# Issuing the first weight load of a decode block ahead of the opening barrier

## The chip, the cores and the metric

The kernel runs on one core of one Trainium2 chip. The metric is the device time of one execution, in microseconds. Times of one set of runs are compared only with the kernel before as it ran in the same set on the same chip.

A ratio of two kernels is the mean time of one kernel's runs over the mean of the other's in the same rounds.

## The reference

The program is one decode step (one token) of a transformer block: layer norm, grouped-query attention over a cache of 65,536 positions, a residual add, then layer norm, a gated GELU feed-forward and a second residual add. All weights and both caches are bfloat16 and are read once.

```python
def _A_ref(x, k_cache, v_cache, wq, wo):          # x is (1, 1, 1024)
    q = (x @ wq).reshape(1, 1, 32, 128).transpose(0, 2, 1, 3)
    k = jnp.repeat(k_cache, 8, axis=1)            # k_cache is (1, 4, 65536, 128)
    v = jnp.repeat(v_cache, 8, axis=1)
    scores = jnp.einsum("bhqd,bhkd->bhqk", q, k) * (128 ** -0.5)
    p = _softmax(scores, axis=-1)
    o = jnp.einsum("bhqk,bhkd->bhqd", p, v)
    return o.transpose(0, 2, 1, 3).reshape(1, 1, 4096) @ wo

def _B_ref(x, w_gate, w_up, w_down):              # 1024 -> 3584 -> 1024
    return (_gelu(x @ w_gate) * (x @ w_up)) @ w_down

h = x + _A_ref(_layernorm(x), A_k_cache, A_v_cache, A_wq, A_wo)
h2 = h + _B_ref(_layernorm(h), B_w_gate, B_w_up, B_w_down)
```

There are about 173 MB to read from HBM, the chip's main memory, and very little arithmetic for each byte.

## The kernel before

All large operands pass through five buffers of 4 MB. SyncE issues every one of these loads; ScalarE issues two small loads of `x`.

```python
    def load(src, name):
        t = chpool.tile([P, CW], BF16, name=name, tag="ch")      # 5 buffers, 128 x 16384 bf16
        n, w = src.shape[1], src.shape[2]
        tv = t[:, 0:n * w].rearrange("p (n w) -> p n w", w=w)
        nc.sync.dma_start(out=tv, in_=src)
        return tv
    # ... cut ...
    nc.scalar.dma_start(out=x_pc_bf[:], in_=A_x[0, 0].rearrange("(p c) -> p c", c=DC))   # 128 x 16 bytes
    nc.scalar.dma_start(out=x_row[:], in_=A_x[0, 0].rearrange("(g n) -> g n", g=4))
    wq_tiles = []
    for c0 in range(0, DC, WB):                                  # two loads of 4 MB
        wv = load(wq_v[:, c0:c0 + WB, :], "wq_sb")
        wq_tiles.extend(wv[:, i, :] for i in range(WB))
    # ... cut: constants, layer norm of x, q = x @ wq, then the K loads, the V loads and the rest ...
```

The kernel already has one build hook, a function that is called with the finished program before it is compiled and may edit its instruction lists (it drops repeated weight loads of TensorE). The change adds a second hook of this kind.

Ahead of the kernel's own instructions the framework puts an opening block. In it GpSimd writes four constants, and then all five engines meet at a barrier: each drains and reports to GpSimd, which releases them. SyncE's part of that block is, in order: drain and report; wait for the release; branch to the body. The first load is the first instruction of SyncE's body and waits for nothing.

## Time and profile before

| What | Value | Read from |
|---|---|---|
| Time, median of 3 runs | 409.46 us | runs |
| Span, first to last instruction | 407.74 us | profile |
| First weight packet starts | 1.76 us | packets in the trace |
| Last weight packet ends | 403.89 us | packets in the trace |
| Stream (the difference) | 402.13 us | |
| Tail after it | 3.84 us | |

A packet is one record of a DMA transfer in the trace; for most of the loads it is the 32 KB row of one partition. "Stream" and "tail" keep the meaning of this table throughout.

The page of the kernel before, its slices, DMA and queue lines. Each digit is the busy share of one fortieth of the span in tenths.

```profile
PE   0455287769998777797966969978767999725464
DVE  0218988876693679545454978181844000220110
DMA  8999999999999999999999999999999999999995
GB/s 360 412 450 424 420 453 411 457 415 447 426 415 460 415 442 428 418 456 415 456 416 421 450 415 455 418 434 437 418 453 418 452 421 431 428 434 436 422 429 222
...
q1 hardware_dynamic: 6488, 173.02, 98.6%
...
HBM read 173.02 MB, written 0.00 MB: 424 GB/s over the span
```

PE and DVE have room in most slices; DMA has none between the first slice and the last. Queue q1 is SyncE's loads.

The stretches table of the kernel before (time in each stretch, busy time and number of instructions of each engine, granted clock, DMA share, GB/s). A short stretch can read above the real rate, because the table books packets whole; so the first rows only show where the DMA starts.

```profile
0.00:1.00 1.00, 0.00 (x0) 0.00 (x0) 0.17 (x2) 0.00 (x0) 0.47 (x6) 1.00 0.00 0
1.00:1.70 0.70, 0.00 (x0) 0.00 (x0) 0.00 (x1) 0.00 (x0) 0.67 (x4) 1.00 0.00 0
1.70:2.70 1.00, 0.00 (x0) 0.00 (x0) 0.00 (x0) 0.90 (x1) 1.00 (x1) 1.00 1.75 524
...
25.00:100.00 75.00, 50.62 (x196) 11.46 (x100) 57.93 (x37) 11.42 (x18) 0.00 (x0) 0.78 1.00 433
100.00:200.00 100.00, 85.85 (x386) 15.26 (x154) 65.50 (x43) 11.53 (x16) 0.00 (x0) 0.98 1.00 432
200.00:300.00 100.00, 80.78 (x331) 13.91 (x131) 59.16 (x40) 11.40 (x16) 1.14 (x2) 0.90 1.00 433
```

No byte moves before 1.70 us, and from 25 us on the share is 1.00 at 432 to 433 GB/s. Counted packet by packet over all queues, the 16 engines were idle for at most 0.1 us per engine between 12 and 395 us. The Trainium skill, "DMA: Bandwidth & Descriptors", section "Where 436 GB/s comes from", puts the ceiling of the fabric at 435 GB/s; this trace is within 1% of it.

The chain of waits of the kernel before seems to tell another story:

```profile
DMA 45%; PE 30%; DVE 18%; ACT 4%; issue 2%; SPq 0%; ACTq 0%; DVEq 0%
```

It follows each load back to the instruction that freed its buffer, and so it wanders through PE and DVE. But such a wait only makes a load enter its queue later, and the queue is never empty: the K loads take 32.9 us from issue to landing (the page's list of issues), while a 4 MB load alone takes 4.19 MB / 432 GB/s = 9.7 us, so about three are queued. Counted from the issues and the packets, the bytes still waiting when a new load is issued are never less than 1.1 loads of 4 MB.

The start of the timeline of the kernel before (start us, us, engine, line, operation, out<-in, count, idle before and its cause; "SPq" and "ACTq" are the issues of SyncE and ScalarE):

```profile
0.24 0.10 POOL L523 MEMSET const-float32-0.0<- 128x1 f32 x1 [0.24 <-issue]
...
0.73 0.41 ACTq L149 DMA_DIRECT2D x_pc_bf<-in_A_x_dram  x1
0.73 0.20 POOL masks.py:197 MEMSET ident_bf<- 128x128 bf16 x1 [0.29 <-POOLq L523]
0.74 0.87 SPq L143 DMA_DIRECT2D wq_sb<-in_A_wq_dram  x2
...
13.07 0.17 DVE L195 CAST x_pc<-x_pc_bf 128x8 f32<-128x8 bf16 x1 [12.07 <-DMA x_pc_bf<-in_A_x_dram]
```

Nothing but constants runs before 0.73 us, when the barrier has let go and both queues issue their first load. The small `x` lands only at 13.07 us. The timeline leaves out the barrier itself; the records of the trace have it (ns from the first instruction):

```
   0  SyncE drains and reports      532  GpSimd has seen all reports
 121  VectorE drains and reports    653  SyncE sees the release
 132  ScalarE drains and reports    736  SyncE starts to issue the first load (393 ns)
 315  TensorE drains and reports   1760  the first packet of that load starts
```

### The profile page before, as it was taken

The page shows a single profiled execution, that of the slowest core. Times are in us where ns is not written, and L with a number is a line of the kernel's source. Part 1 is how long each engine was busy: PE and PEld are TensorE (multiplying, and loading weights), DVE is VectorE, ACT ScalarE, POOL GpSimd, SP SyncE. Part 2 cuts the span into 40 slices and gives each one's busy share as a digit, 9 for nine tenths or more (in the row PEclk, how much of TensorE's full clock was granted, in tenths as well). Part 3 has the DMA queues.
Part 4 walks back from the last instruction along what each step waited for, and adds up shares of the span by engine and source line. Part 5 has one row for each costly group of instructions (what it writes and reads, how often), then busy time and mean ns, then how long its engine had stood idle before and what let it go on. Part 6 is the DMA issues. An engine that isn't in the chain of part 4 may idle for free.

```text
span 407.7 us, 2657 instructions
## 1 busy us (share of the span) xinstructions
PE 298.5 (73%) x1481; PEld 62.8 (15%) x713; DVE 201.9 (50%) x183; ACT 44.9 (11%) x67; POOL 7.4 (2%) x17
## 2 busy tenths in 40 slices
PE   0455287769998777797966969978767999725464
PEld 0121011111111111111101121111112110200232
DVE  0218988876693679545454978181844000220110
ACT  1010000051000041000001420000042000100000
POOL 2000000000000000000000000000010000100000
PEclk9966868969999999899988798999678799875766
DMA  8999999999999999999999999999999999999995
GB/s 360 412 450 424 420 453 411 457 415 447 426 415 460 415 442 428 418 456 415 456 416 421 450 415 455 418 434 437 418 453 418 452 421 431 428 434 436 422 429 222
DMA packets 6652, 173.19 MB, mean 425 GB/s; under 512 B 872, under 2 KB 880, under 8 KB 1136
## 3 DMA queue, kind: packets, MB, share of 16 engines
q1 hardware_dynamic: 6488, 173.02, 98.6%
q8 instruction: 8, 0.13, 0.1%
q10 hardware_dynamic: 152, 0.00, 0.0%
q14 instruction: 4, 0.03, 0.0%
HBM read 173.02 MB, written 0.00 MB: 424 GB/s over the span
## 4 chain that ended last, share of the span: by engine, by line
DMA 45%; PE 30%; DVE 18%; ACT 4%; issue 2%; SPq 0%; ACTq 0%; DVEq 0%
DMA k_sb<-in_A_k_cache_dram 32%; DVE k_sb L255 12%; PE acc_ps L128 12%; DMA wg_sb<-in_B_w_gate_dram 8%; PE qk_ps L126 6%; PE qk_ps L128 6%; DMA wd_sb<-in_B_w_down_dram 5%; PE acc_ps L126 4%; DVE mx L276 2%; ACT sc L275 2%; DVE pT L300 1%; ACT pe_r L297 1%; PE o_ps L126 1%; DVE acc_sb L326 1%; ACT acc_sb L328 1%
## 5 line engine op out<-in xcount | busy, mean ns | idle before, releaser
L255 DVE STREAM_TRANSPOSE k_sb<-k_sb 128x2048 uint32<-128x2048 uint32 x64 | 142.1, 2277 | 33.5 <-DMA k_sb<-in_A_k_cache_dram 33.5
L126 PE MATMUL qk_ps<-k_sb,wsel 128*128 128x512 bf16 x256 | 104.2, 407 | 37.7 <-DVE k_sb L255 24.0
L128 PE MATMUL acc_ps<-v_sb,pT 128*128 128x512 bf16 x384 | 112.3, 404 | 0.0
L128 PE MATMUL qk_ps<-k_sb,wsel 128*128 128x512 bf16 x256 | 103.8, 405 | 0.0
L126 PE MATMUL acc_ps<-v_sb,pT 128*128 128x512 bf16 x128 | 51.8, 405 | 0.0
L126 PEld LDWEIGHTS <-wsel 128*128 128x128 bf16 x256 | 26.1, 102 | 142.7 <-issue 123.6
L276 DVE TENSOR_REDUCE mx<-qk_ps 128x1 f32<-128x1024 f32 x16 | 19.5, 1219 | 45.5 <-ACT sc L275 45.5
L275 ACT COPY sc<-qk_ps 128x1024 f32<-128x1024 f32 x16 | 16.2, 1012 | 202.0 <-PE qk_ps L128 201.9
L126 PEld LDWEIGHTS <-pT 128*128 128x128 bf16 x128 | 13.5, 106 | 99.3 <-issue 99.3
L300 DVE STREAM_TRANSPOSE pT<-pe_r 128x1024 bf16<-128x1024 bf16 x16 | 19.0, 1227 | 6.2 <-ACT pe_r L297 6.2
L326 DVE COPY acc_sb<-acc_ps 32x512 f32<-32x512 f32 x8 | 5.4, 671 | 32.9 <-PE acc_ps L128 32.9
L297 ACT ACTIVATE pe_r<-sc,nbias 128x1024 bf16<-128x1024 f32 x16 | 18.2, 1140 | 14.6 <-DVE nbias L292 13.9
L126 PE MATMUL ln_tot<-ln_s,ones_f 128*128 128x1 f32 x8 | 1.9, 311 | 16.1 <-DVE ln_s L176 14.2
L128 PE MATMUL wu_ps<-wu_sb,hnz 128*32 128x512 bf16 x40 | 7.3, 585 | 7.2 <-DMA wu_sb<-in_B_w_up_dram 7.2
L328 ACT COPY acc_sb<-acc_ps 32x512 f32<-32x512 f32 x8 | 4.6, 578 | 62.1 <-DVE acc_sb L326 62.1
L212 DVE COPY wg_ev<-wg_ps 128x512 f32<-128x512 f32 x1 | 0.7, 692 | 20.0 <-PE wg_ps L126 20.0
L126 PE MATMUL f_ps<-wd_sb,actz 128*32 128x256 bf16 x112 | 6.2, 377 | 5.7 <-DMA wd_sb<-in_B_w_down_dram 5.7
L126 PE MATMUL o_ps<-sel,acc_sb 128*128 128x8 f32 x32 | 5.0, 283 | 6.7 <-DVE rl L340 5.9
L126 PE MATMUL wg_ps<-wg_sb,hnz 128*32 128x512 bf16 x32 | 6.8, 621 | 4.3 <-DMA wg_sb<-in_B_w_gate_dram 2.8
L137 PE MATMUL mxT_ps<-ident_f,mx 128*1 128x128 f32 x4 | 1.4, 346 | 10.8 <-DVE mx L281 10.8
L126 PE MATMUL q_ps<-wq_sb,xnz 128*32 128x512 bf16 x32 | 4.5, 539 | 3.6 <-DMA wq_sb<-in_A_wq_dram 2.0
L126 PEld LDWEIGHTS <-hnz 128*32 128x32 bf16 x48 | 2.7, 129 | 23.4 <-issue 21.8
(100 smaller groups left out, 85.2 us busy)
## 6 DMA issues: line engine op xcount, KB each, us to landing
k_sb<-in_A_k_cache_dram SPq DMA_DIRECT2D x16, 4096.0 KB, 32.9
v_sb<-in_A_v_cache_dram SPq DMA_DIRECT2D x16, 4096.0 KB, 36.8
wq_sb<-in_A_wq_dram SPq DMA_DIRECT2D x2, 4096.0 KB, 16.7
wo_sb<-in_A_wo_dram SPq DMA_DIRECT2D x2, 4096.0 KB, 30.1
wg_sb<-in_B_w_gate_dram SPq DMA_DIRECT2D x2, 3584.0 KB, 31.2
wu_sb<-in_B_w_up_dram SPq DMA_DIRECT2D x2, 3584.0 KB, 32.2
wd_sb<-in_B_w_down_dram SPq DMA_DIRECT2D x1, 3584.0 KB
wd_sb<-in_B_w_down_dram SPq DMA_DIRECT2D x1, 1792.0 KB, 24.4
```

The source lines that it names most:

```text
L126: return pe(t.matmul(out, lhsT=lhsT, rhs=rhs, start=start, stop=stop, tile_position=tile_position, skip_group_check=skip_group_check))
L128: op = t.add_instruction(mybir.InstMatmult(name=nc.get_next_instruction_name(), engine=t.engine, start_tensor_calc=start, stop_tensor_calc ...
L137: pe(nc.tensor.transpose(out=out, in_=in_, identity=identity))
L212: nc.vector.tensor_copy(out=dst, in_=src)
L255: dv(nc.vector.transpose(out=kt[:, c * w:(c + 1) * w], in_=kt[:, c * w:(c + 1) * w]))
L275: ac(nc.scalar.copy(out=sc[:], in_=flat))
L276: dv(nc.vector.tensor_reduce(out=state[("mx", g)][:, li:li + 1], in_=flat, axis=AX.X, op=ALU.max))
L297: ac(nc.scalar.activation(out=pe_r[:], in_=state.pop(("sc", g, li))[:], func=ACT.Exp, bias=nbias[:, 0:1], scale=scale, accum_out=lpart[:, ...
L300: dv(nc.vector.transpose(out=pT[:].rearrange("p m c -> p (m c)"), in_=pe_r[:]))
L326: dv(nc.vector.tensor_copy(out=acc_sb[sl, :], in_=acc[sl, c, :]))
L328: ac(nc.scalar.copy(out=acc_sb[sl, :], in_=acc[sl, c, :]))
```

## The change

The intent is to let the DMA stream start while the engines are still meeting. The first load depends on nothing: its buffer is fresh and it waits for no semaphore. So a hook takes it out of the body and puts it ahead of SyncE's drain in the opening block.

```diff
+    SPE = mybir.EngineType.SP
+
+    def first_load_leads(nc):
+        blocks = nc.m.functions[0].blocks
+        body = next(b for b in blocks if any(isinstance(i, mybir.InstDMACopy) for i in b.instructions))
+        ins = list(body.instructions)
+        at = next(n for n, i in enumerate(ins) if i.engine == SPE)
+        first = ins.pop(at)
+        assert isinstance(first, mybir.InstDMACopy) and not first.sync_info.on_wait
+        head = list(blocks[0].instructions)
+        to = next(n for n, i in enumerate(head) if i.engine == SPE)
+        head.insert(to, first)
+        body.instructions[:] = ins
+        blocks[0].instructions[:] = head
+
+    nc.at_finalize(first_load_leads)
```

No instruction is added or removed. The added source lines shift the line numbers in the profile by 17 (L143 becomes L160, L149 becomes L166).

## The prediction

> **What bounds the kernel now.** The DMA. The page gives 173.02 MB moved at 424 GB/s over a span of 407.7 us, and the slices show DMA at 9 tenths from the second slice to the last but one, PE is busy 73%, DVE 50%. Reading the trace packet by packet: the first weight packet starts at 1.76 us and the last ends at 403.9 us; between those two the 16 engines are together idle for about 1.5 us per engine, nearly all in the first and last 4 us. In the stretches table (25 to 380 us) the DMA share is 1.00 at 431 to 433 GB/s. The Trainium skill, "DMA: Bandwidth & Descriptors", section "Where 436 GB/s comes from", gives 435 GB/s as the fabric ceiling; this trace agrees. Loads take 25 to 37 us from issue to landing, one 4 MB load alone about 10 us, so about three are always queued.
>
> So the span is 1.76 us to the first packet, 402.1 us of stream, and 3.8 us of last matmuls, output and closing barriers.
>
> **What the change does.** In the timeline SyncE is at the opening barrier at 0.00 us (the first engine there), GpSimd has done four memsets and its drain by 0.49 us and sees the gathering complete at 0.53, the release reaches SyncE at 0.65, and the first load is issued at 0.736 (393 ns). Its first packet follows 1.02 us after the issue starts. Moved ahead of the barrier, the issue starts at about 0.00.
>
> - First packet: 1.76 -> about 1.02 us, 0.74 us earlier.
> - Barrier: SyncE arrives after its 0.39 us issue, at 0.40 to 0.45 us; GpSimd needs until 0.53 anyway. So the barrier should not move, unless SyncE's drain waits for descriptors to be written; then by up to 0.5 us.
> - The two small loads of x from ScalarE are still issued at 0.73 and 1.18 us. Their 16-byte packets take turns with the 32 KB weight packets (x_pc_bf lands at 13.0, 12.3 us after issue). I expect x to land 0.7 us earlier with the stream, or up to one 1.24 us packet later relative to it. Either way it costs nothing: the fourth K load, which waits for the first wq buffer, is issued at 20.6 us; the loads ahead of it last until about 49 us.
>
> **How much is on the critical path.** All of it: the stream has no slack. Everything behind the first packet should shift by about 0.7 us. A small extra is possible, because six of the 16 engines get their first weight packet only at 2.1 to 2.7 us, perhaps because x is issued at the same moment (up to 0.2 us).
>
> **Prediction.** 409.46 - 0.74 = 408.7 us (0.18% less), range 408.4 to 409.15. Faster by over 2%: 0.002; within 2%: 0.995; slower by over 2%: 0.003.
>
> **What would show each step right or wrong.** Timeline: SyncE's first instruction is the wq load, at about 0.00 us; GpSimd's barrier release still near 0.6; the second wq load near 0.75. Packets: first wq packet near 1.0 us, last weight packet near 403.1. Stretches: DMA share still 1.00 in the middle, 431 to 433 GB/s. Span about 407.0 us. Tail still 3.8 us.
>
> **What would make it wrong.** The time being counted from something that moves with SyncE's first instruction; SyncE reaching the moved load later than it reached the drain; the barrier being delayed by SyncE; or a stream rate that differs by 0.2% between runs, which would hide or double the gain.

## The result, and the profile after

| | before | after |
|---|---|---|
| Median | 409.47 us (409.42 to 409.67, 4 runs) | 408.73 us (408.67 to 408.85, 4 runs) |
| Ratio | | 0.9981, 95% interval 0.9967 to 0.9995 |
| Span of the profiled run | 407.74 us | 407.06 us |
| First weight packet starts | 1.76 us | 1.03 us |
| Last weight packet ends | 403.89 us | 403.24 us |
| Stream | 402.13 us | 402.21 us |
| Tail | 3.84 us | 3.83 us |
| `x` landed, its cast starts | 13.07 us | 14.56 us |

The kernel is 0.74 us (0.18%) faster. The interval lies below 1. The time isn't merely counted from another point: it exceeds the span by 1.7 us in a run of the kernel before (409.44 and 407.7 us) and by 1.8 us in one of the changed kernel (408.81 and 407.0 us, both of set one below). The page after, the same lines:

```profile
PE   0266286879996789799966969998767997714464
DVE  0218989966573678546464878181853001110110
DMA  9999999999999999999999999999999999999995
GB/s 374 451 412 444 430 425 451 410 451 425 427 448 415 454 417 441 435 412 454 422 443 431 422 445 422 440 435 425 441 422 443 431 422 451 417 432 437 434 416 214
...
q1 hardware_dynamic: 6488, 173.02, 98.7%
...
HBM read 173.02 MB, written 0.00 MB: 425 GB/s over the span
...
DMA 46%; PE 30%; DVE 18%; ACT 4%; issue 1%; SPq 0%; ACTq 0%; DVEq 0%
```

The only slice of DMA that changed is the first, from 8 to 9. The chain of waits is as before. The start of the timeline after:

```profile
0.00 1.14 SPq L160 DMA_DIRECT2D wq_sb<-in_A_wq_dram  x2
0.23 0.10 POOL L540 MEMSET const-float32-0.0<- 128x1 f32 x1 [0.23 <-issue]
...
0.80 0.20 POOL masks.py:197 MEMSET ident_bf<- 128x128 bf16 x1 [0.36 <-POOLq L540]
0.80 0.38 ACTq L166 DMA_DIRECT2D x_pc_bf<-in_A_x_dram  x1
...
14.56 0.17 DVE L212 CAST x_pc<-x_pc_bf 128x8 f32<-128x8 bf16 x1 [13.49 <-DMA x_pc_bf<-in_A_x_dram]
```

SyncE's first load is now the first instruction of all. Everything behind the barrier starts 0.07 us later than before (0.80 instead of 0.73). The records say why: SyncE's drain took 0.007 us before; behind the load it starts at 0.456 us and takes 0.116, so GpSimd has all reports at 0.598 instead of 0.532 us. And the cast of `x` is 1.49 us later. Neither shows in the time.

The stretches after:

```profile
0.00:1.00 1.00, 0.00 (x0) 0.00 (x0) 0.10 (x1) 0.00 (x0) 0.41 (x6) 1.00 0.00 0
1.00:1.70 0.70, 0.00 (x0) 0.00 (x0) 0.07 (x2) 0.00 (x0) 0.66 (x4) 1.00 2.46 702
1.70:2.70 1.00, 0.00 (x0) 0.00 (x0) 0.00 (x0) 0.87 (x1) 1.00 (x2) 1.00 0.08 33
...
25.00:100.00 75.00, 51.03 (x210) 10.72 (x103) 60.86 (x38) 11.41 (x18) 0.00 (x0) 0.86 1.00 433
100.00:200.00 100.00, 87.54 (x375) 16.16 (x151) 62.91 (x43) 11.97 (x16) 0.00 (x0) 0.93 1.00 431
200.00:300.00 100.00, 81.19 (x332) 14.46 (x135) 59.73 (x44) 10.96 (x15) 1.14 (x2) 0.90 1.01 435
```

The first bytes moved from the stretch 1.70 to 2.70 into the one before it. The rate in the long stretches is the same, so what was gained at the start is still there at the end.

### The profile page after: what moved, and what is told of

It reads as the page before. It is cut to its first block, busy times and chain, and to the rows that moved or that the text cites. A ratio compares the mean times of both kernels' runs of the same rounds, so it can differ in the third digit from the quotient of the medians.

```text
span 407.1 us, 2657 instructions
## 1 busy us (share of the span) xinstructions
PE 298.8 (73%) x1481; PEld 64.1 (16%) x713; DVE 202.0 (50%) x183; ACT 44.9 (11%) x67; POOL 7.4 (2%) x17
## 4 chain that ended last, share of the span: by engine, by line
DMA 46%; PE 30%; DVE 18%; ACT 4%; issue 1%; SPq 0%; ACTq 0%; DVEq 0%
DMA k_sb<-in_A_k_cache_dram 32%; DVE k_sb L272 12%; PE acc_ps L145 12%; DMA wg_sb<-in_B_w_gate_dram 9%; PE qk_ps L143 6%; PE qk_ps L145 6%; DMA wd_sb<-in_B_w_down_dram 5%; PE acc_ps L143 4%; DVE mx L293 3%; ACT sc L292 2%; DVE pT L317 1%; ACT pe_r L314 1%; PE o_ps L143 1%; DVE acc_sb L343 1%; ACT acc_sb L345 1%
## 5 line engine op out<-in xcount | busy, mean ns | idle before, releaser
L143 PE MATMUL qk_ps<-k_sb,wsel 128*128 128x512 bf16 x256 | 103.7, 405 | 34.7 <-DVE k_sb L272 21.3
L145 PE MATMUL acc_ps<-v_sb,pT 128*128 128x512 bf16 x384 | 114.3, 410 | 0.0
L143 PE MATMUL acc_ps<-v_sb,pT 128*128 128x512 bf16 x128 | 52.9, 413 | 0.0
L143 PEld LDWEIGHTS <-wsel 128*128 128x128 bf16 x256 | 26.0, 101 | 138.3 <-issue 118.2
L143 PEld LDWEIGHTS <-pT 128*128 128x128 bf16 x128 | 13.8, 108 | 101.9 <-issue 101.9
L143 PE MATMUL ln_tot<-ln_s,ones_f 128*128 128x1 f32 x8 | 1.9, 311 | 17.6 <-DVE ln_s L193 15.7
L145 PE MATMUL wu_ps<-wu_sb,hnz 128*32 128x512 bf16 x40 | 6.4, 524 | 7.5 <-DMA wu_sb<-in_B_w_up_dram 7.5
L143 PE MATMUL o_ps<-sel,acc_sb 128*128 128x8 f32 x32 | 6.6, 335 | 6.7 <-DVE rl L357 6.3
L229 DVE COPY wg_ev<-wg_ps 128x512 f32<-128x512 f32 x1 | 0.7, 692 | 20.6 <-PE wg_ps L143 20.6
L143 PE MATMUL f_ps<-wd_sb,actz 128*32 128x256 bf16 x112 | 6.9, 415 | 5.4 <-DMA wd_sb<-in_B_w_down_dram 5.3
L143 PE MATMUL wg_ps<-wg_sb,hnz 128*32 128x512 bf16 x32 | 5.3, 488 | 6.7 <-DMA wg_sb<-in_B_w_gate_dram 6.7
L143 PEld LDWEIGHTS o_ps<-sel,acc_sb 128*128 128x128 f32 x32 | 6.3, 293 | 7.0 <-issue 6.0
```

What stands on the lines that cost most here:

```text
L143: return pe(t.matmul(out, lhsT=lhsT, rhs=rhs, start=start, stop=stop, tile_position=tile_position, skip_group_check=skip_group_check))
L145: op = t.add_instruction(mybir.InstMatmult(name=nc.get_next_instruction_name(), engine=t.engine, start_tensor_calc=start, stop_tensor_calc ...
L229: nc.vector.tensor_copy(out=dst, in_=src)
```

## The experiments

The theory: the DMA stream bounds the whole program and has no gap in which a later start could hide, so the time follows the start of the first weight packet one for one, and nothing else that the change touched matters. The rivals: that the difference is scatter; that it comes from the barrier or from an earlier start of the other engines; and that the early issue as such helps, whatever it carries. Twelve kernels were run in three sets of four; all gave the correct result. "Before" in a set is the median of nine runs.

### Set one: the change again, and two kinds of delay (before: 409.55 us)

**The changed kernel itself**, without an edit.

> The changed kernel itself, once more, beside the kernel before on the same chip. Theory (the DMA stream bounds the whole program and is shifted as a block): 0.65 to 0.80 us less than before, first weight packet near 1.03 us, stream of 402.1 to 402.3 us, tail 3.8 us. Rival (the difference is scatter between executions or chips): the intervals of the two overlap, differences of either sign.

Measured: 408.81 us (408.70 to 408.96, 5 runs), 0.74 us less, ratio 0.9982 (0.9969 to 0.9994). First packet at 1.03 us, stream 402.12 us, tail 3.83 us. No run of the changed kernel was as slow as the fastest run of before (409.40). It is not scatter.

**One weight load held.** A GpSimd memset writes into the first load's buffer, so that the load must wait for it.

```diff
+        if not held:
+            held.append(nc.gpsimd.memset(t[:, 0:2080], 0.0))     # the long hold: 0:8320
         nc.sync.dma_start(out=tv, in_=src)
```

> The kernel before, with its first weight load made to wait for a GpSimd memset of 2080 columns (1.82 us in the trace of before) that writes into the load's buffer. First issue then near 2.65 us instead of 0.74, so +1.9 us. Theory (stream shifted as a block, one for one): 411.2 to 411.5 us. Rival (the change gains by taking the barrier's or SyncE's work off a chain of instructions, and the stream has slack in which a later start is hidden): less than +0.5 us.

> The same with a memset of 8320 columns (estimate 7.3 us from four times 1.82): first issue near 8.1 us, +7.4 us. Theory: 416.5 to 417.2 us, a slope of 1.0 against the short hold. Rival with slack: the second dose costs less per us, or the first costs nothing.

Measured: 409.43 us and 409.58 us; ratios 0.9998 (0.9984 to 1.0012) and 1.0000 (0.9988 to 1.0013). That looks like the rival, but the edit had not done what was meant. SyncE's issues in the timeline of the long hold:

```profile
0.74 7.38 SPq L147 DMA_DIRECT2D wq_sb<-in_A_wq_dram  x2
8.16 0.93 SPq L147 DMA_DIRECT2D k_sb<-in_A_k_cache_dram  x2
```

The first line is a merged row of two issues. The framework's scheduler had put the other half of `wq`, which waits for nothing, in front; it was issued at 0.74 us as ever, and only the second load was held, until 7.79 us. The first packet started at 1.75 us in both kernels. The numbers of both expectations are therefore not tested. What the long hold does show is another point of the theory: the second load can come 6.6 us late (7.79 instead of 1.19 us), and the first query matmul 5.3 us late (22.5 instead of 17.2 us), at no cost, as long as something is in the queue.

**The load of `x` held instead**: four GpSimd memsets and a copy into its buffer.

```diff
+    for _ in range(4):
+        nc.gpsimd.memset(wsel[:], 0.0)
+    nc.gpsimd.tensor_copy(out=x_pc_bf[:], in_=wsel[:, 0:DC])
     nc.scalar.dma_start(out=x_pc_bf[:], in_=A_x[0, 0].rearrange("(p c) -> p c", c=DC))
```

> The kernel before, with the first small load of x made to wait for four GpSimd memsets and a copy (about 7.4 us) instead; the weight loads are left alone. x should land between 19 and 23 us instead of 13.1, the first query matmul and the release of the first weight buffer follow 6 to 10 us later than before. Theory: the time stays within 0.2 us of before, as the queued loads last to about 49 us. Rival (what counts is how early the first computation can start): +6 us or more.

Measured: 409.46 us, ratio 1.0000 (0.9987 to 1.0012). From its timeline:

```profile
9.10 0.37 ACTq L152 DMA_DIRECT2D x_pc_bf<-in_A_x_dram  x1
...
22.69 0.17 DVE L198 CAST x_pc<-x_pc_bf 128x8 f32<-128x8 bf16 x1 [12.84 <-DMA x_pc_bf<-in_A_x_dram]
```

The cast came 9.6 us later than before, and the load that reuses the first weight buffer was issued at 30.3 instead of 20.6 us. Nothing of it arrived at the end. So the 1.49 us by which the change delays `x` are free, and an earlier start of the first computation is not where the gain comes from.

### Set two: the whole stream held, and more moved ahead (before: 409.63 us)

**The whole stream held.** The same memset, with SyncE's loads kept in program order by scheduling dependences, so that none can pass the held one. Without the memset that is the order which the kernel before has anyway; that version was not run by itself.

```diff
+        if "sp" not in latest:
+            nc.gpsimd.memset(t[:, 0:2080], 0.0)                  # the long hold: 0:8320
-        nc.sync.dma_start(out=tv, in_=src)
+        keep(nc.sync.dma_start(out=tv, in_=src), "sp")
```

> The kernel before with SyncE's loads kept in program order and the first of them made to wait for a GpSimd memset of 2080 columns into its buffer, so that the whole SyncE stream is held (the earlier hold only moved the second load). First issue near 2.6 us instead of 0.74, +1.9 us; the x loads then find idle engines and land by 4 us, which may give back 0.1 to 0.2 us. Theory (stream shifted as a block): 1.6 to 2.0 us more than before, first weight packet near 3.6 us, stream 402.0 to 402.3 us. Rival (the stream has slack that hides a later start, or the gain came from the barrier): less than +0.5 us.

> The same with 8320 columns (7.03 us in the run before): first issue near 7.8 us, +7.05 us. Theory: 6.7 to 7.1 us more than before, that is 5.0 to 5.3 us more than the short hold. Rival: clearly less than the added hold.

The timeline of the long hold:

```profile
0.73 7.03 POOL L144 MEMSET wq_sb<- 128x8320 bf16 x1 [0.29 <-POOLq L525]
...
7.79 0.86 SPq L145 DMA_DIRECT2D wq_sb<-in_A_wq_dram  x2
8.70 1.50 SPq L145 DMA_DIRECT2D k_sb<-in_A_k_cache_dram  x3
```

| | first weight packet | stream | tail | time | against before |
|---|---|---|---|---|---|
| before (profile: first section) | 1.76 us | 402.13 us | 3.84 us | 409.63 us | |
| short hold | 3.60 us (+1.84) | 402.16 us | 3.82 us | 411.27 us | +1.64 us, ratio 1.0045 (1.0031 to 1.0058) |
| long hold | 8.81 us (+7.05) | 402.20 us | 3.84 us | 416.57 us | +6.94 us, ratio 1.0171 (1.0157 to 1.0185) |

From the short hold to the long one the packet moved by 5.21 us and the time by 5.30. In the profiles the spans grew by 1.85 us (407.74 to 409.59) and 7.12 us (to 414.86). That is one for one, in the direction opposite to the change and ten times as far, with the barrier left where it was. Both medians are 0.1 to 0.2 us below the shift of the packet. The expectation had allowed for that, because the tiny packets of `x` find idle engines here instead of mixing with the weights; but the streams are not shorter (402.16 and 402.20 us), so it may as well be scatter: in the ten profiled runs whose loads were not split, the stream lies between 401.96 and 402.44 us.

**All five free loads ahead of the barrier.**

```diff
-        at = next(n for n, i in enumerate(ins) if i.engine == SPE)
-        first = ins.pop(at)
-        assert isinstance(first, mybir.InstDMACopy) and not first.sync_info.on_wait
+        firsts = [i for i in ins if i.engine == SPE][:5]
+        assert all(isinstance(i, mybir.InstDMACopy) and not i.sync_info.on_wait for i in firsts)
+        ins = [i for i in ins if i not in firsts]
-        head.insert(to, first)
+        head[to:to] = firsts
```

> The change extended: all five loads that wait for nothing go ahead of SyncE's opening barrier. SyncE then reaches the barrier after five issues (about 2.2 us), so every other engine and the x loads start about 1.7 us later than in the changed kernel. Theory (only the first packet's time counts): the same as the changed kernel within 0.15 us, that is 0.6 to 0.9 us less than before. Rival (the start of the other engines counts too): 1 us or more above the changed kernel.

Measured: 408.83 us, 0.80 us less than before, ratio 0.9983 (0.9970 to 0.9995). From its timeline:

```profile
0.00 0.87 SPq L160 DMA_DIRECT2D wq_sb<-in_A_wq_dram  x2
...
0.91 1.49 SPq L160 DMA_DIRECT2D k_sb<-in_A_k_cache_dram  x3
2.81 0.40 ACTq L166 DMA_DIRECT2D x_pc_bf<-in_A_x_dram  x1
```

The other engines left the barrier at 2.81 us instead of 0.80, and the time is that of the changed kernel to within what can be told apart. This takes the barrier out of the question: 2 us of it cost nothing. It also says that moving more than one load is of no use.

**The loads of `x` ahead as well**, on ScalarE's side of the opening block.

```diff
     nc.at_finalize(first_load_leads)
+    # x_leads: the same edit for ScalarE, with its first two instructions (the loads of x)
+    nc.at_finalize(x_leads)
```

> The changed kernel with ScalarE's two loads of x moved ahead of its opening barrier as well. The barrier will be up to 0.6 us later, as ScalarE's two issues take 1.0 us; x should land 1 to 3 us earlier than the 14.6 us of the changed kernel. Theory: the same as the changed kernel within 0.15 us, as x is off the critical path. Rival (x and the first layer norm count): 0.5 us or more below the changed kernel.

Measured: 408.86 us, 0.77 us less than before, ratio 0.9983 (0.9971 to 0.9996). The cast of `x` began at 12.36 us, 2.2 us earlier than in the changed kernel, and gained nothing. (The barrier came 0.75 us later, a little more than the 0.6 us allowed for.)

### Set three: how much has to be ahead (before: 409.56 us)

If only bytes count, a lead of few bytes should gain little. The first load was split by partitions, and only a part went ahead.

```diff
+        if "sp" not in latest:
+            for r, c in [(slice(0, 16), slice(0, 1)), (slice(0, 16), slice(1, n)), (slice(16, P), slice(0, n))]:
+                keep(nc.sync.dma_start(out=tv[r, c, :], in_=src[r, c, :]), "sp")
+        else:
+            keep(nc.sync.dma_start(out=tv, in_=src), "sp")
-        nc.sync.dma_start(out=tv, in_=src)
```

This is the 128 KB lead (with the hook of the change) and its control (without the hook). The 512 KB lead takes all columns of the 16 partitions at once; the 16 KB lead takes their first 512 columns.

> The changed kernel with its first weight load split by partitions: 16 partitions (512 KB, one 32 KB packet for each of the 16 engines) go ahead of the barrier, the other 112 after it. One packet took 1.7 us at the start in the changed kernel, longer than the wait for the barrier, so the engines should not run dry. Theory: the same as the changed kernel, 0.6 to 0.9 us less than before. If issue and first packet depend on the number of packets described, the first packet comes before 1.03 us and the kernel is up to 0.2 us below the changed one. Rival (the whole load must be ahead): clearly less gain.

> As above, but only 128 KB (16 partitions of 8 KB) go ahead, the rest in two loads after the barrier. 128 KB are 0.30 us of a stream of 430 GB/s. Theory (what counts is the bytes moved before the stream would have started): 0.2 to 0.5 us less than the same split without the early issue, unless the latency of the first packet (about 0.5 us of its 1.7) is also paid early, then up to 0.75. Rival (the early issue itself, not its bytes, gives the gain): 0.7 us or more, as the full load.

> The same split without the early issue: the control for the 128 KB lead. Theory: the same as before within 0.2 us, perhaps up to 0.2 us more as the second issue follows a packet of only 0.3 us.

> Only 16 KB (16 partitions of 1 KB) go ahead, 0.04 us of the stream, the rest in three loads after the barrier. Theory by bytes: within 0.15 us of the control, so no gain from an early issue as such. Rival (an early first packet wakes the engines and that is the gain): 0.5 us or more less than the control.

| | time | against before | against the control | first packet |
|---|---|---|---|---|
| control: split, no lead | 418.65 us | +9.09 us, ratio 1.0222 | | 1.79 us |
| 16 KB lead | 418.58 us | +9.02 us, ratio 1.0221 | -0.07 us | 1.03 us |
| 128 KB lead | 417.91 us | +8.35 us, ratio 1.0203 | -0.74 us | 1.04 us |
| 512 KB lead | 418.31 us | +8.75 us, ratio 1.0211 | (other split) | 1.03 us |

The control and the 512 KB lead missed their expected times by about 9 us, and the two leads that were to be compared with the control lie 9 us above before with it: the split itself costs that. In the stretches of the control the lost time is all at the start:

```profile
4.00:13.00 9.00, 1.17 (x4) 1.00 (x4) 2.49 (x17) 0.00 (x0) 0.82 (x2) 1.00 0.98 233
13.00:22.00 9.00, 0.00 (x0) 0.00 (x0) 0.00 (x0) 0.00 (x0) 0.00 (x0) 1.00 0.90 233
22.00:40.00 18.00, 9.68 (x76) 3.20 (x44) 1.08 (x3) 1.01 (x3) 0.00 (x0) 1.00 1.01 437
```

The same stretches of the kernel before:

```profile
4.00:13.00 9.00, 0.00 (x0) 0.00 (x0) 0.00 (x0) 0.00 (x0) 0.00 (x0) 1.00 0.95 408
13.00:22.00 9.00, 4.55 (x36) 1.74 (x21) 2.49 (x17) 0.00 (x0) 0.82 (x2) 1.00 1.02 441
```

The engines are as busy as ever but move 233 GB/s instead of 408 to 441. In the packets, 32 KB took 2.8 us on average at 4 to 6 us and still 2.1 us at 18 to 20 us; 1.21 us is the usual figure. Nearly all of this is the divided load: by 22 us 4.19 MB had moved, which is what it holds, its last part landed at 21.2 to 22.3 us, and the undivided load behind it landed 9.7 us later, at full rate. A likely cause is stated by the Trainium skill, "SBUF — State Buffer", section "Door 1: The DMA port swizzle": "DMA bandwidth depends on how many of the 16 SBUF ports your partitions reach"; by its table partitions 0 to 15 reach only four. The direction agrees (the first 32 KB packets of the 512 KB lead took 3.7 us, those of the changed kernel 1.8), but no run here varied the partitions alone, so the cause is argued, not shown. It also covers less than half of the loss. In the control the 16 partitions (0.52 MB) took about 5.3 us, some 4 us more than at 432 GB/s. The 112 others (3.67 MB) took about 14.4 us, some 6 us too many, although by the same table they leave no port out. Why they were slow stays open. The small packets are not needed for it: the 512 KB lead moved rows of 32 KB alone and lost as much.

What the set still says, within its family: a lead of 16 KB brought the first packet from 1.79 to 1.03 us, as the change does, and gained 0.07 us, which is within scatter. So an early issue as such was worth nothing that this set can see. The packets say why: the early ones were through by 1.5 us, and the next weight packet started at 1.77 us, where the control's first one starts at 1.79. The lead of 128 KB gained 0.74 us, at the upper end of what was expected, and also over the 0.7 us named for the rival, so by itself it doesn't decide. As an estimate, at the 233 GB/s of this stage 131 KB are worth 0.56 us, so the bytes would account for most of it, but with the stage so disturbed the amount is not a clean test. A split by columns over all 128 partitions would have been the better edit; it was not run. The 512 KB lead did not improve on the changed kernel and, at +8.75 us, is no candidate.

No version beat the changed kernel: moving more loads or `x` ahead equals it, and splitting the load loses 9 us.

## Why the prediction was right

- **What bounds the kernel.** Right, and shown by the holds: 1.84 us and 7.05 us of later first packet cost 1.64 and 6.94 us, while 9.6 us of later `x` and 6.6 us of later second load cost nothing. Two readings in it were loose. The 1.5 us of idle engines counts weight packets alone, and 0.6 us of it lies in the middle, where the engines mostly fetch instructions instead. And "about three are always queued" is the rule, not the least: that is 1.1.
- **The size.** "1.76 -> about 1.02 us, 0.74 us earlier" was measured as 1.76 to 1.03 us, 0.73 us earlier. The issue started at 0.00 us, and the packet followed 1.03 us after it; before it was 1.02 us. The time fell by 0.74 us in two separate sets, to 408.73 us against 408.7 predicted.
- **All of it on the critical path.** Right: stream 402.13 and 402.21 us, tail 3.84 and 3.83 us.
- **The barrier.** "should not move, unless SyncE's drain waits for descriptors to be written". It moved by 0.07 us, because the drain behind the load took 0.116 us. SyncE had reported at 0.57 us, not at 0.40 to 0.45. That is inside the stated allowance and costs nothing: with all five loads ahead the barrier moved by 2 us, also for nothing.
- **The loads of `x`.** This step was off. The prediction had `x` land 0.7 us earlier, "or up to one 1.24 us packet later relative to" the stream. It landed 1.49 us later in absolute terms, 2.2 us later relative to the stream, which is nearly two packets of 1.21 us. Before, the first `x` packet went at 3.56 us, as soon as the first weight packet was through; after, at 5.17 us, when three were through. So the term that was mis-sized is the number of weight packets that pass first: two more than before, where the prediction allowed one. The conclusion that it costs nothing held, as three runs show (`x` cast at 12.36, 17.02 and 22.69 us with no effect on the time).
- **The small extra from a more even start.** Not found. The first packets of the 16 engines start between 1.03 and 1.95 us after, 1.76 and 2.66 us before: the same spread. (In the repeat they start between 1.03 and 1.56 us, at the same time of the kernel.) The gain is 0.74 us without it.

## What to carry to other kernels

Where the DMA stream has no gap from its first packet to its last, as in this kernel, the time follows the first packet one for one; so look at what stands between the first instruction and the first packet, and move one load that depends on nothing, and that is large enough to cover the wait, ahead of it. Before adding more, ask what is in the queue: with more than one load always queued, neither later issues, nor a later barrier, nor a later first computation showed here. When an edit is meant to delay one instruction, check in the timeline that the scheduler didn't let another pass it.

## What the Trainium skill lacked or had wrong

- "DMA: Bandwidth & Descriptors", section "Specifications", gives a first-byte latency of about 0.6 us for loads issued by SyncE and ScalarE, but not from where it counts. Here the first packet starts 1.02 to 1.03 us after the issue starts; taken from the end of the 0.39 us issue it is 0.63 us, which agrees.
- The same page, section "Where 436 GB/s comes from", says that for transfers between HBM and SBUF the HBM side, about 358 GB/s, binds. With one core running, these traces hold 430 to 435 GB/s from HBM for hundreds of microseconds, close to the fabric figure of the same section. The sentence lacks its condition: the note under the page's table of measured rates gives about 358 GB/s as the share of each core when both cores of the HBM domain stream, which no run here did.
- The same page, section "Queues, rings and completion order", has each engine take turns between queues packet by packet, but not how many packets of a running queue pass before a newcomer gets its first turn. Here it was one weight packet when both queues were issued together, three when the weights had a lead of 0.8 us, and four with a lead of 2.8 us (all five loads ahead); the first `x` packet went at 3.56, 5.17 and 6.52 us. On idle engines it went 1.0 us after its issue (the held streams).
- "SBUF — State Buffer", section "Door 1: The DMA port swizzle", fits the slow load to 16 partitions (0.52 MB in about 5.3 us), but not the load to the other 112 behind it, which leaves no port out by its table and took about 14.4 us for 3.67 MB (255 GB/s). The full 128-partition load after that ran at full rate (9.7 us).
- No page has the opening barrier that the framework puts into the program: 0.65 us until SyncE is released, and a drain that grows from 0.007 to 0.116 us when a load was issued just before it.
